# A two-branch linear-attention kernel: folded weights laid by branch, K's PSUM as two tiles, and another order of the first steps

## The chip, the cores and the metric

The kernel runs on one core of a Trainium2 chip. The metric is the device time of one execution in microseconds (us). PE is the matrix engine (PEld its weight loads), DVE the vector engine, ACT the scalar engine, POOL the GpSimd engine, and SP issues the transfers. SBUF is the on-chip memory, PSUM the matrix engine's output memory, eight banks of 512 float32 a partition.

## The reference

Two branches, A and B, of the same form work on the same x (2048 tokens, 448 features, 16 heads of 28). A gate mixes their outputs.

```python
qkv = (x @ wqkv).reshape(B, S, 3, H, Dh).transpose(2, 0, 3, 1, 4)
q, k, v = qkv[0], qkv[1], qkv[2]
pq = einsum("bhsd,hdf->bhsf", q, w_phi)
pk = einsum("bhsd,hdf->bhsf", k, w_phi)
phi_q = concatenate([softmax(pq), softmax(-pq)], -1)
phi_k = concatenate([softmax(pk), softmax(-pk)], -1)
kv = einsum("bhsf,bhsd->bhfd", phi_k, v)
z = einsum("bhsf->bhf", phi_k)
o = einsum("bhqf,bhfd->bhqd", phi_q, kv) / (einsum("bhqf,bhf->bhq", phi_q, z) + 1e-6)
branch = o.transpose(0, 2, 1, 3).reshape(B, S, D) @ wo
out = g * A + (1 - g) * B        # g = sigmoid((x * gate_w).sum(-1))
```

## The kernel before

The 2048 tokens are 16 tiles of 128 (`t`), loaded two at a time. Matrix products are made from a high and a low part of each operand: x, the V weights and the folded weights are each split into a rounded copy ("high", by ACT) and what is left over (`low_part`, a subtraction on DVE or POOL). A projection of one tile and one branch is then 11 matmuls into one PSUM bank (`mms`): the high x with the high and the low weights in four chunks each, and three packed chunks of the low x with the high weights. The order `XT` puts high times high first, the low weights from the fifth matmul, and the low x last.

**Warm-up.** `warm` (L638) issues 10 large and 30 small matmuls of zeros, each of which shows as two instructions in the trace.

**V of tiles 0 and 1.** `v_first` takes the chunks in the order in which they come in. The steps that feed it are `load_x0`, `split_x0`, `load_wv` and `split_wv`. V's banks are VA and VB; tile 1 uses K's two banks instead (`v_bank`).

**Folds.** K and Q go straight from x to the features, so the products of `wqkv` and `w_phi` are made on the chip, in four steps F0 to F3 (`fold(n, low)`: branch `b` is n // 2, `gh` is n % 2). One fold is 32 small matmuls into the four-bank tile F, a transpose by DVE to SBUF, which frees F for the next fold, and then four times (K and Q, chunks `j` 0 and 2) a high copy by ACT and a low part by DVE ("D") or POOL ("P"). Each fold is preceded by `load_wt`: eight transfers on SP and a copy on POOL whose key is `wd`. The results lie in `rk` and `rq`, in which chunk, branch and feature are the axes in this order, and are `wkh`, `wkl`, `wqh`, `wql`.

**The body.** K of a tile (`k_proj` for each branch, `k_soft`) goes to the tile "K" of two PSUM banks, one per branch, and is copied by ACT to SBUF (`pk`). DVE takes the maximum and the minimum, POOL subtracts, ACT takes the exponentials, DVE sums and takes reciprocals, and POOL multiplies. Q (`q_proj`, `q_front`, `q_soft`) goes to the tile "Q"; DVE subtracts the maximum, and the result goes through DRAM to a form in which DVE transposes it. `kv_acc` adds the states of two tiles (T0), V's copies lie in `vs`. At the end the kernel makes the numerators (`num`), divides, gates, and multiplies by `wo` (`out_mm`).

**What sets the order.** The steps are added to a planner (`Plan`) in the order of the generator `steps()`. PE's own order is the order in which its steps are added. For the other engines `order()` makes a list schedule with a cost for each step: a step's due time is the earliest due time of those that need it, less its cost, less its argument `ahead`; of the steps that are ready on an engine the one with the earliest due time goes first. `ahead` is passed on to the steps before it. What the engines then do on the chip is in the planned order, whatever their real times are. The order of the first steps stands in `steps()`, L111 to L114:

```python
    yield from (("V", 3, 0), ("F", 1, "DP"), ("V", 3, 1), ("F", 2, "DP"), ("V", 4, 0), ("F", 3, "DP"), ("later",), ("k", 0, 0), ("V", 4, 1), ("q", 0, 0), ("k", 0, 1), ("ks", 0))
    yield from (("K", 1), ("wo_rows",), ("q", 0, 1), ("qf", 0))
    yield from (("S", 0, JIT % 3 - 1), ("K", 2), ("Q", 1), ("S", 1, (JIT - 1) % 3 - 1), ("k", 3, 0), ("k", 3, 1), ("kv", 0, 1), ("ks", 3), ("V", 5))
```

"V" is a tile's V projection with its copies, "k" one branch of a K projection, "ks" the K features of a tile, "q" and "qf" the same for Q, "S" the second half of Q's features, "kv" the states. `later` closes F and opens the banks of Q, of T0 and of O0.

Most operations are recorded at a helper's line: L266 is `tt` (a two-operand operation of DVE or POOL), L269 `act`, L272 `dma`, L410 the matmuls of `mms`.

Of the kernel before, what the change touches and what calls it, by code (L numbers as in the profile page):

```python
# [10 lines left out]
OP = mybir.AluOpType  # L11
# [13 lines left out]
WARM, SMALL = 10, 30  # L25


class Plan:
# [8 lines left out]
    def add(self, eng, cost, fn, r=(), w=(), lat=0.1, kb=0, two=None, ahead=0.0):  # L37
# [10 lines left out]
        self.steps.append((eng, cost, lat, fn, deps, kb, eng == "POOL" if two is None else two, ahead))  # L48
# [4 lines left out]
    def order(self):  # L53
# [19 lines left out]
        for _ in range(n):  # L73
# [10 lines left out]
            i = min((i for i in can[eng] if ready[i] <= t), key=lambda i: due[i])  # L84
            can[eng].remove(i)
            _, cost, lat, _, _, kb, two, _ = self.steps[i]
# [83 lines left out]
def hedgehog_mix(ctx: ExitStack, tc: tile.TileContext, xd, wv, wkt, wqt, wphi, wo, cmask, cpmask, out):  # L170
# [42 lines left out]
    banks("kv", "left", K=2, VA=1, VB=1)  # L213
# [8 lines left out]
    wkh, wkl = (rk[:, i].rearrange("p (c b f h) -> p c b f h", c=4, b=2, f=FD) for i in range(2))  # L222
    wqh, wql = (rq[:, i].rearrange("p (c b f h) -> p c b f h", c=4, b=2, f=FD) for i in range(2))
# [100 lines left out]
    def split_wv(c, b, low):  # L324
# [4 lines left out]
        low_part(low, D, l, wvr[:, c, lo:hi], h.bitcast(F32), [("wvr", c, b), ("vh", c, b)], [("vl", c, b)], ahead=600.0 - 100 * c if b == 0 else 0.0)  # L329
# [21 lines left out]
    def fold(n, low):  # L351
# [13 lines left out]
        for k, (wh, wl) in enumerate(((wkh, wkl), (wqh, wql))):  # L365
            for j in (0, 2):
                h, l = (x[:, j:j + 2, b, :, gh::2].rearrange("p j f u -> p j u f") for x in (wh, wl))
                s = f[:, k, j:j + 2, :FD].rearrange("p j f u -> p j u f")
                key = "kq"[k]
                add("ACT", 0.9, act(h, s), [ftk[n % 2]], [(key, "h", b, gh, j)], ahead=2.0 * (k == 0))  # L370
                e = "POOL" if low[k] == "P" or low[k] == "M" and j else "DVE"
                add(e, {"DVE": 0.88, "POOL": 1.4}[e], tt(e, l, s, h.bitcast(F32), OP.subtract), [ftk[n % 2], (key, "h", b, gh, j)], [(key, "l", b, gh, j)], two=False)
# [43 lines left out]
    def feat(w, b):  # L416
        return [x[:, :, b].rearrange("p c f h -> p c (f h)") for x in w]
# [7 lines left out]
    def v_bank(t, b):  # L425
        return ("K", b, ("K", b)) if t == 1 else (("VA", "VB")[b], 0, ("VA", "VB")[b])
# [20 lines left out]
    def v_proj(t, b):  # L447
# [4 lines left out]
        v_out(t, b)  # L452
# [9 lines left out]
    def k_proj(t, b):  # L462
        add("PE", 11 * 0.197, mms(t, feat((wkh, wkl), b), "K", b, FO, FZ),
            xkeys(t) + wkeys("k", (b,)), [("K", b)])

    def k_soft(t):
        def p4():
            return fm(bank["K"][:, :, FO:FO + D])
# [13 lines left out]
        put("DVE", 2 * D, lambda: V.tensor_reduce(mh[0], pkh, AX.X, OP.max), [kp], [km[0]])  # L482
        put("DVE", 2 * D, lambda: V.tensor_reduce(mh[1], pkh, AX.X, OP.min), [kp], [km[1]])
        put("POOL", 2 * D, tt("POOL", e4[0], pkh, bc[0], OP.subtract), [kp, km[0]], [ke[0]])
        put("POOL", 2 * D, tt("POOL", e4[1], bc[1], pkh, OP.subtract), [kp, km[1]], [ke[1]])
        for s in range(2):
# [3 lines left out]
            add("DVE", 0.25, lambda s=s: V.reciprocal(sm[:, s], sm[:, s]), [], [("sm", t % 2, s)])  # L490
# [172 lines left out]
    first("DVE", 0.1, lambda: V.memset(bank["K"][:, :, FZ:FZ + H], 0.0), [("K", 0), ("K", 1)])  # L663
# [7 lines left out]
    def later():  # L671
# [10 lines left out]
        for i in range(1, 3):  # L682
            first("POOL", 0.4, lambda i=i: G.memset(eqs[i][:, :, :, :, DH:], 0.0), turned(i - 1))
# [10 lines left out]
    for what, *a in steps():  # L694
        if what == "V":
            for b in a[1:] or (0, 1):
                v_proj(a[0], b)
        elif what == "V01":
# [113 lines left out]
```

## Time and profile before

| | us |
|---|---|
| median of three runs | 342.83 (342.69 to 345.25) |
| the profiled execution | 342.14 |
| its span in the trace | 340.4 |
| PE busy | 332.1 |
| DVE busy | 279.6 |
| POOL busy | 252.2 |
| ACT busy | 143.3 |

The span is what the trace shows from the first instruction to the last; 1.7 us of the execution lie around it. A group of matmuls overlaps in the array, so a group's busy time includes the tail of its last matmul. In the trace the names of tiles stand without their numbers, and an SBUF tile may hold several things in turn: `ret` holds the V weights as loaded, the raw weights of the folds, the K features and the Q features.

### The profile page before, as it was taken

How to read it: one execution, taken by the hardware profiler on the slowest of the kernel's cores; microseconds unless marked ns; L12 is line 12 of the kernel's file. 1: busy time of each engine (PE TensorE's matmuls, PEld its weight loads, DVE VectorE, ACT ScalarE, POOL GpSimd, SP SyncE). 2: the span in 40 equal slices, each digit the busy share in tenths (PEclk: the TensorE clock that was granted, in tenths of full speed). 3: DMA queues.
4: the chain of work that ended last, by engine and by line, in shares of the span. 5: the costliest groups of instructions: out<-in, count | busy, mean ns of one | idle time of the engine just before them, and what ended most of it. 6: DMA issues, size and time to landing. Idle time of an engine off the chain costs nothing.

```text
span 340.4 us, 8927 instructions
## 1 busy us (share of the span) xinstructions
PE 332.1 (98%) x3776; PEld 296.1 (87%) x3776; DVE 279.6 (82%) x335; ACT 143.3 (42%) x219; POOL 252.2 (74%) x212
## 2 busy tenths in 40 slices
PE   8999999999999999999999999999899999999995
PEld 8877889899999999999999998899678888888895
DVE  4547839986797789899988989985799999999970
ACT  4647634462454463546426244342043343433231
POOL 7158365999999799999967985993088778788500
PEclk9999999999999999999999999999999999999999
DMA  7887503612349639848364232396855545241011
GB/s 252 257 212 207 149 1 72 202 56 74 97 158 325 170 107 341 276 145 302 98 221 169 66 111 62 102 351 206 307 178 172 199 156 166 91 179 56 30 54 54
DMA packets 29855, 54.73 MB, mean 161 GB/s; under 512 B 4616, under 2 KB 25464, under 8 KB 27512
## 3 DMA queue, kind: packets, MB, share of 16 engines
q1 hardware_dynamic: 29560, 54.06, 49.1%
q8 instruction: 29, 0.48, 0.6%
q0 software_dynamic: 256, 0.12, 0.1%
q14 instruction: 10, 0.08, 0.1%
HBM read 31.54 MB, written 24.22 MB: 164 GB/s over the span
## 4 chain that ended last, share of the span: by engine, by line
PE 44%; POOL 24%; DVE 14%; issue 9%; DMA 5%; ACT 3%; SPq 1%; POOLq 0%; DVEq 0%; ACTq 0%
PE O L631 21%; POOL ret L266 20%; PE N L583 7%; PE Q L410 5%; PE VB L410 3%; POOL rx L266 3%; PE K L410 3%; DVE ret L546 3%; DVE sm L489 2%; PE VA L410 2%; DVE mx L482 2%; DMA ed<-ret 2%; DMA ret<-in_wv 2%; PE F L358 1%; ACT ret L269 1%
## 5 line engine op out<-in xcount | busy, mean ns | idle before, releaser
L410 PE MATMUL K<-rk,rx 128*128 128x432 f32 x352 | 72.5, 360 | 0.7 <-ACT pk L269 0.6
L410 PE MATMUL Q<-rq,rx 128*128 128x432 f32 x352 | 72.5, 360 | 0.3 <-DVE ru L266 0.3
L631 PE MATMUL O<-rk,rx 128*128 128x448 f32 x336 | 70.4, 368 | 0.0
L410 PEld LDWEIGHTS K<-rk,rx 128*128 128x128 f32 x352 | 65.7, 188 | 5.1 <-ACT pk L269 1.5
L410 PEld LDWEIGHTS Q<-rq,rx 128*128 128x128 f32 x352 | 65.8, 188 | 4.7 <-DVE ru L266 0.9
L631 PEld LDWEIGHTS O<-rk,rx 128*128 128x128 f32 x336 | 62.6, 188 | 8.1 <-issue 1.2
L269 ACT ACTIVATE ret<-ret 128x896 f32<-128x896 f32 x48 | 45.7, 953 | 56.2 <-POOL ret L266 56.0
L266 POOL TENSOR_TENSOR ret<-ret,sm 128x896 f32<-128x896 f32 x32 | 53.9, 1704 | 9.5 <-DVE sm L490 9.5
L489 DVE TENSOR_REDUCE sm<-ret 128x32 f32<-128x896 f32 x32 | 33.8, 1075 | 8.6 <-ACT ret L269 8.6
L546 DVE STREAM_TRANSPOSE ret<-ret 128x2048 f32<-128x2048 f32 x16 | 36.5, 2281 | 1.8 <-POOL ret L266 1.4
L541 DVE TENSOR_REDUCE qsm<-ret 128x32 f32<-128x896 f32 x32 | 33.4, 1053 | 2.7 <-ACT ret L269 2.4
L410 PE MATMUL VA<-rv,rx 128*128 128x450 f32 x154 | 34.4, 371 | 0.0
L410 PE MATMUL VB<-rv,rx 128*128 128x448 f32 x154 | 33.7, 366 | 0.0
L266 POOL TENSOR_TENSOR ret<-qmn,ru 128x896 f32<-128x896 f32 x16 | 28.2, 1762 | 6.9 <-DVE ret L546 4.2
L410 PEld LDWEIGHTS VB<-rv,rx 128*128 128x128 f32 x154 | 28.8, 188 | 3.0 <-issue 0.8
L269 ACT ACTIVATE ret<-ru 128x896 f32<-128x896 f32 x16 | 15.2, 950 | 38.3 <-issue 18.9
L410 PEld LDWEIGHTS VA<-rv,rx 128*128 128x128 f32 x154 | 28.6, 189 | 2.9 <-ACT rk L269 0.4
L266 POOL TENSOR_TENSOR ret<-pk,mx 128x896 f32<-128x896 f32 x16 | 27.3, 1704 | 4.8 <-DVE mx L482 4.7
L266 POOL TENSOR_TENSOR ret<-ret,qsm 128x896 f32<-128x896 f32 x16 | 27.2, 1702 | 0.9
L266 POOL TENSOR_TENSOR ret<-mx,pk 128x896 f32<-128x896 f32 x16 | 27.3, 1705 | 0.0
L603 POOL TENSOR_TENSOR rv<-rv,rd 128x896 f32<-128x896 f32 x14 | 23.8, 1703 | 1.1
L583 PE MATMUL N<-ret,kvt 32*32 32x256 f32 x1024 | 22.7, 385 | 1.6 <-issue 1.6
(92 smaller groups left out, 435.9 us busy)
## 6 DMA issues: line engine op xcount, KB each, us to landing
ed<-ret SPq DMA_DIRECT2D x8, 1024.0 KB
ret<-ed SPq DMA_DIRECT2D x8, 1024.0 KB
qd<-ru SPq DMA_DIRECT2D x64, 112.0 KB
ru<-qd SPq DMA_DIRECT2D x16, 448.0 KB
out<-ret SPq DMA_DIRECT2D x16, 224.0 KB
wod<-wst SPq DMA_DIRECT2D x14, 224.0 KB
rk<-wod SPq DMA_DIRECT2D x2, 1568.0 KB
xraw<-in_xt SPq DMA_DIRECT2D x6, 512.0 KB
```

The lines of the kernel that those rows point to most:

```text
L266: return lambda: ENG[eng].tensor_tensor(val(o), val(a), val(b), op)
L269: return lambda: A.activation(val(o), val(i), f, **k)
L358: nc.tensor.matmul(bank["F"][32 * o:32 * o + 32, q, 256 * l:256 * l + 256], wpd[32 * q:32 * q + DH, b, g], wts[32 * q:32 * q + DH, :, b, g ...
L410: nc.tensor.matmul(bank[name][:, k, lo:hi], x[:, xc, o:o + P], w[l][:, c], start=i == 0, stop=i == len(XT) - 1)
L482: put("DVE", 2 * D, lambda: V.tensor_reduce(mh[0], pkh, AX.X, OP.max), [kp], [km[0]])
L489: put("DVE", 2 * D, lambda s=s, e3=e3: V.tensor_reduce(sm[:, s], e3, AX.X, OP.add), [ke[s]], [("sm", t % 2, s)])
L541: put("DVE", 2 * D, lambda s=s, e3=e3: V.tensor_reduce(qsm[:, s], e3, AX.X, OP.add), [ke[s]], [("qsm", i, s)])
L546: add("DVE", 2.25, lambda: V.transpose(eTf[slot], eq.rearrange("p s a c f -> p (s a c f)")), ke, turned(slot))
L583: nc.tensor.matmul(bank["N"][32 * g:32 * g + 32, r, 2 * b * P:2 * b * P + 2 * P], kvt[32 * r:32 * r + 32, b, s, g], eTp[slots[0] // 2][32 ...
L603: put(eng, 2 * D, lambda: ENG[eng].tensor_tensor(mid["o", n % 3].rearrange("p (c a f) -> p a c f", c=4, a=8), ctv()[:, :, i, :, :DH], rd[: ...
L631: nc.tensor.matmul(bank[pb][:, 0, :D], a, w, start=i == 0, stop=i == len(terms) - 1)
```

## The change

- **Warm-up:** 11 large and 15 small matmuls in place of 10 and 30.
- **Layout:** `rk` and `rq` hold branch, chunk, feature in place of chunk, branch, feature. The slices in `fold` and `feat` follow.
- **K's PSUM:** two tiles of one bank, K0 and K1, in place of one of two banks. `k_soft` copies each branch by itself, for every tile; before, this was so for tile 0 alone.
- **Planner:** a new argument `now` moves a step forward among the ready ones, but is not passed on to the steps before it. The reciprocals of the K sums of tiles 0 and 1 have `now` 20 and 12.
- **First steps:** other `ahead` values for the low parts of x's first two tiles and of V's weights.
- **Folds:** in F1 the low K part of chunk 0 goes to POOL ("N"); F0's low Q part of chunk 2 stays behind `wd` 2; the two memsets of `eqs` on POOL come behind `wd` 3.
- **Order on PE:** V of tile 4, branch 1, goes ahead of K of tile 0, branch 0; V of tile 5, branch 0, goes ahead of the states of tiles 0 and 1, and its copies behind them ("vm" is the projection, "vo" the copies).

```diff
-WARM, SMALL = 10, 30
+WARM, SMALL = 11, 15
...
-            i = min((i for i in can[eng] if ready[i] <= t), key=lambda i: due[i])
+            i = min((i for i in can[eng] if ready[i] <= t), key=lambda i: due[i] - self.steps[i][8])
...
-    yield from (("V", 3, 0), ("F", 1, "DP"), ("V", 3, 1), ("F", 2, "DP"), ("V", 4, 0), ("F", 3, "DP"), ("later",), ("k", 0, 0), ("V", 4, 1), ("q", 0, 0), ("k", 0, 1), ("ks", 0))
+    yield from (("V", 3, 0), ("F", 1, "NP"), ("V", 3, 1), ("F", 2, "DP"), ("V", 4, 0), ("F", 3, "DP"), ("later",), ("V", 4, 1), ("k", 0, 0), ("q", 0, 0), ("k", 0, 1), ("ks", 0))
...
-    yield from (("S", 0, JIT % 3 - 1), ("K", 2), ("Q", 1), ("S", 1, (JIT - 1) % 3 - 1), ("k", 3, 0), ("k", 3, 1), ("kv", 0, 1), ("ks", 3), ("V", 5))
+    yield from (("S", 0, JIT % 3 - 1), ("K", 2), ("Q", 1), ("S", 1, (JIT - 1) % 3 - 1), ("k", 3, 0), ("k", 3, 1), ("vm", 5, 0), ("kv", 0, 1), ("vo", 5, 0), ("ks", 3), ("V", 5, 1))
...
-    banks("kv", "left", K=2, VA=1, VB=1)
+    banks("kv", "left", K0=1, K1=1, VA=1, VB=1)
...
-    wkh, wkl = (rk[:, i].rearrange("p (c b f h) -> p c b f h", c=4, b=2, f=FD) for i in range(2))
+    wkh, wkl = (rk[:, i].rearrange("p (b c f h) -> p b c f h", c=4, b=2, f=FD) for i in range(2))
...
-        low_part("DVE", 2 * P, t[:, 4], xraw[:, 0], f[:, 0], [("x0raw", 0), ("x0h", 0)], [("x0l", 0)], ahead=165.0)
+        low_part("DVE", 2 * P, t[:, 4], xraw[:, 0], f[:, 0], [("x0raw", 0), ("x0h", 0)], [("x0l", 0)], ahead=680.0)
...
-        low_part("DVE", 2 * P, t[64:P, 3], xraw[64:P, 3], f[64:P, 3], [("x0raw", 1)], [("x0h", 3)], ahead=135.0)
-        low_part("DVE", 4 * P, t[:, 5:7], xraw[:, 1:3], f[:, 1:3], [("x0raw", 1), ("x0h", 1), ("x0h", 2)], [("x0l", i) for i in (1, 2)], ahead=140.0)
+        low_part("DVE", 2 * P, t[64:P, 3], xraw[64:P, 3], f[64:P, 3], [("x0raw", 1)], [("x0h", 3)], ahead=660.0)
+        low_part("DVE", 4 * P, t[:, 5:7], xraw[:, 1:3], f[:, 1:3], [("x0raw", 1), ("x0h", 1), ("x0h", 2)], [("x0l", i) for i in (1, 2)], ahead=440.0)
...
-        low_part(low, D, l, wvr[:, c, lo:hi], h.bitcast(F32), [("wvr", c, b), ("vh", c, b)], [("vl", c, b)], ahead=600.0 - 100 * c if b == 0 else 0.0)
+        low_part(low, D, l, wvr[:, c, lo:hi], h.bitcast(F32), [("wvr", c, b), ("vh", c, b)], [("vl", c, b)], ahead=(600.0, 600.0, 400.0, 300.0)[c] if b == 0 else 0.0)
...
-                e = "POOL" if low[k] == "P" or low[k] == "M" and j else "DVE"
+                e = "POOL" if low[k] == "P" or low[k] == "N" and j == 0 else "DVE"
...
-        if t:
-            put("ACT", 2 * D, act(pk, p4), [("K", 0), ("K", 1)], [kp])
-        else:
-            for b in range(2):
-                put("ACT", D, act(pk[:, b], lambda b=b: p4()[:, b]), [("K", b)], [("pk0", b)])
-            plan.hand_over([("pk0", b) for b in range(2)], [kp])
+        for b in range(2):
+            put("ACT", D, act(pk[:, b:b + 1], lambda b=b: fm(bank[f"K{b}"][:, :, FO:FO + D])), [("K", b)], [(*kp, b)])
+        kp = [(*kp, b) for b in range(2)]
...
-            add("DVE", 0.25, lambda s=s: V.reciprocal(sm[:, s], sm[:, s]), [], [("sm", t % 2, s)])
+            add("DVE", 0.25, lambda s=s: V.reciprocal(sm[:, s], sm[:, s]), [], [("sm", t % 2, s)], now=(20.0, 12.0)[t] if t < 2 else 0.0)
...
-            first("POOL", 0.4, lambda i=i: G.memset(eqs[i][:, :, :, :, DH:], 0.0), turned(i - 1))
+            add("POOL", 0.4, lambda i=i: G.memset(eqs[i][:, :, :, :, DH:], 0.0), [("wd", 3)], turned(i - 1))
```

More of the change, by code (lines that the diff above doesn't have):

```diff
@@ L35, in __init__, with add @@
         self.steps, self.writer, self.readers = [], {}, {}
-    def add(self, eng, cost, fn, r=(), w=(), lat=0.1, kb=0, two=None, ahead=0.0):
+    def add(self, eng, cost, fn, r=(), w=(), lat=0.1, kb=0, two=None, ahead=0.0, now=0.0):
         i, deps = len(self.steps), set()
@@ L47, in add @@
             self.writer[k], self.readers[k] = i, set()
-        self.steps.append((eng, cost, lat, fn, deps, kb, eng == "POOL" if two is None else two, ahead))
+        self.steps.append((eng, cost, lat, fn, deps, kb, eng == "POOL" if two is None else two, ahead, now))
     def hand_over(self, old, new, fn=None):
@@ L83, in order @@
             t, eng = best
-            i = min((i for i in can[eng] if ready[i] <= t), key=lambda i: due[i])
+            i = min((i for i in can[eng] if ready[i] <= t), key=lambda i: due[i] - self.steps[i][8])
             can[eng].remove(i)
-            _, cost, lat, _, _, kb, two, _ = self.steps[i]
+            _, cost, lat, _, _, kb, two, _, _ = self.steps[i]
             if two:
@@ L416, in feat @@
     def feat(w, b):
-        return [x[:, :, b].rearrange("p c f h -> p c (f h)") for x in w]
+        return [x[:, b].rearrange("p c f h -> p c (f h)") for x in w]
     def hb(ap):
@@ L425, in v_bank @@
     def v_bank(t, b):
-        return ("K", b, ("K", b)) if t == 1 else (("VA", "VB")[b], 0, ("VA", "VB")[b])
+        return (f"K{b}", 0, ("K", b)) if t == 1 else (("VA", "VB")[b], 0, ("VA", "VB")[b])
     def v_weights(b):
@@ L662, in hedgehog_mix @@
     load_x(1)
-    first("DVE", 0.1, lambda: V.memset(bank["K"][:, :, FZ:FZ + H], 0.0), [("K", 0), ("K", 1)])
+    for b in range(2):
+        first("DVE", 0.1, lambda b=b: V.memset(bank[f"K{b}"][:, :, FZ:FZ + H], 0.0), [("K", b)])
     for i, v in enumerate(vs):
@@ L697, in hedgehog_mix @@
                 v_proj(a[0], b)
+                v_out(a[0], b)
+        elif what in ("vm", "vo"):
+            (v_proj if what == "vm" else v_out)(*a)
         elif what == "V01":
```

21 lines of the change are left out of this document (9 added, 12 removed).

## The prediction

> **What bounds the kernel now.** I read the summary of the page first, then the waits of PE, then two stretches of the table by stretch, then the timeline of the first 70 us.
>
> ```profile
> span 340.4 us, 8927 instructions
> PE 332.1 (98%) x3776; PEld 296.1 (87%) x3776; DVE 279.6 (82%) x335; ACT 143.3 (42%) x219; POOL 252.2 (74%) x212
> PE N L583 <- issue: 1.6, 2, 1.0
> PE K L410 <- ACT pk L269: 0.6, 1, 0.6
> PE F L358 <- DVE ret L363: 0.5, 1, 0.5
> PE T L501 <- POOL ret L266: 0.4, 2, 0.2
> PE VA L442 <- DVE rx L266: 0.3, 1, 0.3
> PE Q L410 <- DVE ru L266: 0.3, 1, 0.3
> 46.00:59.00 13.00, 12.35 (x60) 11.19 (x61) 10.56 (x13) 6.30 (x8) 7.85 (x5) 1.00 0.17 39
> 59.00:172.00 113.00, 112.78 (x1160) 105.26 (x1159) 98.85 (x118) 54.03 (x76) 109.07 (x75) 1.00 0.56 181
> ```
>
> PE is busy for 332.1 of 340.4 us. A wait row gives its total, how often and the longest: here is everything PE waited for after its first instruction, some 3.7 us in six places. So the change cannot win more than these, the extra cost that each leaves behind, and what it saves at the start. The last two rows give, by stretch, the busy time of PE, PEld, DVE, ACT, POOL (count in brackets), then granted clock, DMA share and GB/s. From 59 to 172 us PE idles 0.2 us, but POOL is busy for 109.07 of 113 us as well: two engines are full, and whoever brings PE forward must bring POOL forward too. From 46 to 59 us POOL works only 7.85 of 13 us; there it has 5.15 us to give.
>
> **The change part by part.** A timeline row is start, busy time, engine, line, operation, tiles, count, and in brackets the idle time before and its releaser. The start:
>
> ```profile
> 1.06 4.62 PE L640 MATMUL VB<-zero 128*128 128x128 f32 x20 [1.06 <-DVE zero L649]
> 5.61 0.72 PE L643 MATMUL F<-zero 32*32 32x32 f32 x60
> 6.26 0.47 PE L442 MATMUL VA<-rv,rx 128*128 128x450 f32 x1
> 6.97 0.63 DVE L266 TENSOR_TENSOR rv<-ret,rv 128x450 fp32r<-128x450 f32 x1 [0.68 <-ACT rv L269]
> 9.43 0.36 PE L442 MATMUL K<-rv,rx 128*128 128x450 f32 x1
> 9.52 0.42 DVE L266 TENSOR_TENSOR rx<-xraw,rx 64x256 fp32r<-64x256 f32 x1
> 10.09 0.44 PE L442 MATMUL VA<-rv,rx 128*128 128x450 f32 x1 [0.29 <-DVE rx L266]
> 11.40 2.39 PE L442 MATMUL VB<-rv,rx 128*128 128x448 f32 x11
> ```
>
> *Warm-up.* The 10 large matmuls are 20 instructions from 1.06 to 5.61, 0.23 each; one more adds 0.46 if at that pace. The 30 small are 60 instructions in 0.65; fifteen fewer save about 0.33. Sum +0.13, V01 starting at 6.39; ends: -0.33 (the large one free) and +0.46 (the small ones hide under something); I take the proportional value.
>
> [...]
>
> *Order of the x and V splits.* V01's 16 matmuls from 6.26 to 9.43 go at one each 0.2 us; the next comes only at 10.09, 0.66 later, because DVE makes the low half of x's fourth chunk last, at 9.52. With `ahead` 660 that step goes ahead of V's low parts, behind the copy it needs; DVE has 0.68 us idle ahead of 6.97, and the step takes 0.42. Next late is V's chunk 3, whose low part DVE does behind 6.97, in the row order now two steps before 9.52, so at 9.5; the matmul that needs it comes after 10. Gain 0.46; ends 0 (the planner puts it elsewhere) and 0.6.
>
> ```profile
> 28.15 1.79 PE L358 MATMUL F<-ret,wpd 28*32 28x256 f32 x64
> 29.63 0.93 DVE L266 TENSOR_TENSOR rk<-ru,rk 128x432 fp32r<-128x432 f32 x1 [1.53 <-ACT rk L269]
> 29.87 2.50 PE L410 MATMUL VA<-rv,rx 128*128 128x450 f32 x11
> 30.46 2.31 DVE L363 STREAM_TRANSPOSE ret<-F 128x2048 f32<-128x2048 f32 x1
> 31.18 2.66 POOL L266 TENSOR_TENSOR rq<-ru,rq 128x432 fp32r<-128x432 f32 x2 [0.36 <-ACT rq L269]
> 32.70 1.93 DVE L266 TENSOR_TENSOR rk<-ru,rk 128x432 fp32r<-128x432 f32 x1
> 32.83 1.79 PE L358 MATMUL F<-ret,wpd 28*32 28x256 f32 x64 [0.46 <-DVE ret L363]
> 34.55 2.44 PE L410 MATMUL K<-rk,rx 128*128 128x432 f32 x11
> 39.52 1.67 DVE L266 TENSOR_TENSOR rk<-ru,rk 128x432 fp32r<-128x432 f32 x2
> 41.45 4.47 PE L410 MATMUL K<-rk,rx 128*128 128x432 f32 x22
> 42.49 2.65 POOL L266 TENSOR_TENSOR rq<-ru,rq 128x432 fp32r<-128x432 f32 x2 [4.31 <-ACT rq L269]
> ```
>
> *Folds.* F3 (32.83) waits for the transpose of F2, which starts at 30.46 although F2's matmuls end at 29.87: DVE is on F1's first K low part (0.93). "NP" gives that part to POOL, so the transpose starts near 29.95 and ends 2.31 later, at 32.26: F3 0.5 earlier. V4's first half ends at about 32.2 and is late next, so no more than 0.6; the other end is 0, should DVE still have another part there. POOL gets one 1.33 us operation (2.66 for two). It delays F1's Q parts on POOL, which nobody reads before Q0, behind K0's first half (34.55) and V4's second. DVE's 0.93 becomes 1.93 while POOL's pair runs, so the two engines do hold each other up: one more POOL part can cost DVE up to 1.33. DVE's last K parts (39.52, done at 41.19) are read by the K matmuls from 41.45, which will come about 1 us sooner, but their low halves only from the fifth of eleven matmuls, 0.8 later, and DVE has shed 0.93. I take 0; ends -0 and +0.8. [...]
>
> The two memsets of `eqs` and the fold's copy `wd 2` only change places in POOL's queue; none of the moved steps issues a transfer on SP or POOL. POOL idles 4.3 us ahead of 42.49, which hides them; without that cover they cost at most their length. Putting V4's second half ahead of K0 is neutral in work; it hides the last folds better: 0.2 from the restarts between 34.55 and 41.45 (ends 0 and 0.3).
>
> ```profile
> 41.45 1.75 ACT L269 ACTIVATE rq<-ru 128x432 fp32r<-128x432 f32 x2 [2.01 <-PE Q L410]
> 45.96 0.54 ACT L269 ACTIVATE pk<-K 128x448 f32<-128x448 f32 x1 [2.38 <-PE K L410]
> 46.54 1.09 DVE L482 TENSOR_REDUCE mx<-pk 128x32 f32<-128x896 f32 x1 [5.35 <-ACT pk L269]
> 46.56 2.47 PE L410 MATMUL K<-rk,rx 128*128 128x432 f32 x11 [0.63 <-ACT pk L269]
> 50.36 0.90 ACT L269 ACTIVATE pk<-K 128x896 f32<-128x896 f32 x1
> 55.80 4.59 PE L410 MATMUL Q<-rq,rx 128*128 128x432 f32 x22
> 58.64 0.98 DVE L490 RECIPROCAL sm<-sm 128x32 f32<-128x32 f32 x4
> 59.13 6.68 POOL L266 TENSOR_TENSOR ret<-ret,sm 128x896 f32<-128x896 f32 x4 [2.00 <-DVE sm L490]
> 65.87 0.99 PE L501 MATMUL T<-ret,vs 128*29 128x56 f32 x64 [0.22 <-POOL ret L266]
> 66.79 2.53 PE L410 MATMUL VA<-rv,rx 128*128 128x450 f32 x11
> 207.96 4.59 PE L410 MATMUL Q<-rq,rx 128*128 128x432 f32 x22 [0.27 <-DVE ru L266]
> ```
>
> *Two K tiles.* K0's second half ends near 43.6, but ACT's copy of it starts at 45.96, when the K matmuls of tile 1 in the other bank are done too: with one tile of two banks the copy waits for both. So the 22 matmuls from 41.45 take until 46.56, 5.11 us. They are busy for 4.47, of which the last one's tail of some 0.16 (0.36 busy against 0.2 a step, the row at 9.43) could overlap the next: 4.31. With two tiles the copy starts near 43.7, and the wait goes: 0.8, and I add 0.1 for the slower first matmul after a wait, 0.9; ends 0.6 (the wait's own row) and 1.0. It also starts the whole chain of tile 0 (46.54) 2.2 us sooner, with the shift 3 or more. Later tiles pay two copies of 0.54 for one of 0.90, 0.18 on ACT, which is 42% busy: nothing on PE, if the half copies hold nobody up behind them (a rival).
>
> *Then.* K2 at 51.31 and Q1 at 55.80 come behind short restarts for the copy at 50.36 and DVE's Q front; both releasers come 2 to 3 us sooner: 0.5 together; ends 0 and 0.6.
>
> *Fold layout.* ACT's last Q parts wait 2.01 for PE's Q matmuls of the other branch, which are interleaved with them in one range; laid by branch they need not. POOL, 4.31 idle, gets them sooner. Nobody waits for the result: 0. Copies and operands have the same shapes.
>
> *Reciprocals first, V5 ahead of kv.* Four reciprocals run together at 58.64, POOL idling 2.00 for them; with `now` they follow their sums, and POOL's four products (6.68) end 4 us sooner, near 62. V5's first half ahead of the states gives 2.2 more. The state stall (0.22, with restart 0.4) goes; ends 0.2 and 0.4. Next late would be the Q front, if DVE did the sums first.
>
> **Sum.** +0.13 - 0.46 - 0.5 - 0.2 - 0.9 - 0.5 - 0.4 = -2.83 us at 66.79; behind it nothing changes if POOL moves along, and N's 1.6 of "issue" stays. The profiled execution took 342.14 us (span 340.4) and would take 339.3; the median of the runs is 342.83, 0.69 above it, so 340.0.
>
> **The rivals.**
> *More than that.* POOL gains more (about 4) than PE (2.8), so the late waits at 207.96 (0.27, with restart 0.4) and at the states near 216 (0.2, with restart 0.4) go too. For it: both wait on the DVE and POOL chain that the change starts earlier. Against: between 172 and 207 that chain already has slack, and the order there is planned anew. 340.0 - 0.8 = 339.2.
>
> *Given back.* POOL, full from 59 to 172, doesn't start earlier after all (its products keep waiting for DVE's sums), and PE arrives earlier only to wait at the states. Then V01 and the folds bring nothing behind 60 us; up to 2.4 of the gain is lost: 341 to 342.6. Against: POOL's 5.15 idle us.
>
> *Slower.* In-order ACT stands at a half copy for a K bank while an exponential that POOL's full queue needs stands behind it. A half is 2.2 us of matmuls; at 0.5 us for each of 13 tiles from tile 3 on, 6.5 are lost against 2.8: 346.5. It decides from 0.22 a tile upwards. Against: ACT has half its time free.
>
> *Clock.* V01 runs at half clock if the clock rises later: 22 matmuls at 0.2 more, +4.4, 344.4. Against: the warm-up is no shorter. [...]
>
> **How the numbers follow.** Forecast 0.41 (own range 339.3 to 340.7), more than that 0.29, given back 0.21, slower 0.06, clock 0.03. A measurement of this kernel tells about 1% from no change, 3.4 us: 339.4 is the line. Faster by over 1% is "more" and a few hundredths of the forecast, 0.33; slower by over 1% 0.06; the rest 0.61. The range takes in "more" with the warm-up's lower end, 338.7, and "given back" to 342.4; it leaves out the last two rivals and the edges.
>
> **What would show it.** V01 without a gap; F3 without its wait; the second K copy right behind the second half of K0, and no PE wait on it; reciprocals apart; no wait at the states. The forecast is wrong if PE shows new waits behind 66 us, for POOL or the Q front, or if F3's wait stays.

## The result, and the profile after

The diff above is an excerpt. Of what it leaves out, one line that the list above it doesn't name sets an order: in `fold` the high copies of K have `ahead` 6.0 in place of 2.0. No run varies that line alone.

| | before | after |
|---|---|---|
| median of 14 runs each, us | 342.73 (340.85 to 345.25) | 339.68 (338.24 to 341.85) |
| the profiled execution | 342.14 | 339.24 |
| its span | 340.4 | 337.4 |

The ratio of the times is 0.992, 95% interval 0.9896 to 0.9945: 2.7 us less, by less than 1%. The prediction said 340.0 for the median and 339.3 for the profiled execution. But the 2.9 us of the trace came in other places than the prediction had them, so the places come first.

From the page of the changed kernel, the summary, and then from its waits of PE (total, times, longest):

```profile
span 337.4 us, 8903 instructions
PE 329.8 (98%) x3748; PEld 296.6 (88%) x3748; DVE 279.2 (83%) x335; ACT 144.4 (43%) x234; POOL 254.7 (75%) x213
PE Q L410 <- DVE Q L672: 1.2, 1, 1.2
PE O L625 <- issue: 1.0, 1, 1.0
PE Q L410 <- DVE ru L266: 0.8, 1, 0.8
```

Of the six waits of before, those on `pk`, on the transpose `ret`, on `ret` at the states and on `rx` are gone. The wait for a Q front has grown from 0.3 to 0.8, "issue" has fallen from 1.6 to 1.0, and the longest, at L672, is new.

Where PE stands at the same piece of work is read from the starts in the two timelines. The last column sums the prediction's terms up to that point.

| PE's work | before | after | difference | predicted |
|---|---|---|---|---|
| VB behind `v_first` | 11.40 | 11.03 | -0.37 | -0.33 |
| F3 | 32.83 | 32.05 | -0.78 | -0.83 |
| Q of tile 0, first branch ("Q0") | 39.22 | 39.68 | +0.46 | -1.03 |
| Q, second branch, behind 33 matmuls of K | 48.86 | 48.38 | -0.48 | -1.93 |
| K of tile 3 | 60.23 | 59.15 | -1.08 | -2.43 |
| K behind the first states | 71.38 | 69.85 | -1.53 | -2.83 |
| Q of the wait `ru` ("the late Q") | 207.96 | 206.89 | -1.07 | -2.83 |
| K behind the states near 215 | 216.83 | 215.34 | -1.49 | -2.83 |
| first N | 238.63 | 237.10 | -1.53 | -2.83 |
| second N | 247.40 | 244.29 | -3.11 | -2.83 |
| last O | 319.50 | 316.55 | -2.95 | -2.83 |

The first 70 us brought 1.5 us, not 2.8, and the loss stands in one line, between F3 and Q0 (1.24 lost where 0.2 was to be won). The other half of the gain came at the first N, where the prediction had nothing.

The start and the folds, from the timeline of the changed kernel (start, busy, engine, line, operation, tiles, count, and in brackets the idle time before and its releaser):

```profile
5.87 0.86 DVE L266 TENSOR_TENSOR rx<-xraw,rx 128x256 fp32r<-128x256 f32 x2
6.39 0.51 PE L442 MATMUL VA<-rv,rx 128*128 128x450 f32 x1
...
30.97 3.37 POOL L266 TENSOR_TENSOR rq<-ru,rq 128x432 fp32r<-128x432 f32 x2
31.92 1.20 DVE L266 TENSOR_TENSOR rk<-ru,rk 128x432 fp32r<-128x432 f32 x1
32.05 1.79 PE L358 MATMUL F<-ret,wpd 28*32 28x256 f32 x64
33.05 4.10 DVE L266 TENSOR_TENSOR rk<-ret,rk 128x432 fp32r<-128x432 f32 x2
34.80 3.59 POOL L266 TENSOR_TENSOR rq<-ret,rq 128x432 fp32r<-128x432 f32 x2
37.06 2.30 DVE L363 STREAM_TRANSPOSE ru<-F 128x2048 f32<-128x2048 f32 x1
39.45 0.09 DVE L672 MEMSET Q<- 128x32 f32 x1
39.68 2.40 PE L410 MATMUL Q<-rq,rx 128*128 128x432 f32 x11 [1.25 <-DVE Q L672]
41.91 6.62 PE L410 MATMUL K<-rk,rx 128*128 128x432 f32 x33
```

The fourth chunk of x now stands in the pair at 5.87, and V01 runs without its gap. F3 runs without its wait. But behind it DVE makes the two K low parts of F2 (33.05), which take 4.10 where one alone takes 0.93 (in the trace of before the two of F2 took 0.95 and 1.34, the second one behind F3's transpose), while POOL's pairs beside them take 3.37 and 3.59 instead of 2.66: each engine is held up while the other works. F3 was done at 33.84 and its transpose begins only at 37.06. F's banks are Q's banks: the zeros of Q wait for that transpose, and Q0 for the zeros. From 41.91 the 33 K matmuls run through; before, 22 and 11 of them stood around a wait of 0.63.

The first states and the late Q in the changed kernel, and two stretches of its table by stretch (length, busy time of PE, PEld, DVE, ACT, POOL, then granted clock, DMA share, GB/s):

```profile
56.48 5.14 POOL L266 TENSOR_TENSOR ret<-ret,sm 128x896 f32<-128x896 f32 x3
65.81 1.78 PE L495 MATMUL T<-ret,vs 128*29 128x56 f32 x128
206.89 4.56 PE L410 MATMUL Q<-rq,rx 128*128 128x432 f32 x22 [0.82 <-DVE ru L266]
46.00:59.00 13.00, 13.00 (x68) 12.46 (x68) 10.65 (x14) 6.47 (x10) 10.92 (x7) 1.00 0.21 57
59.00:172.00 113.00, 113.00 (x1162) 105.64 (x1161) 97.47 (x118) 54.43 (x85) 105.53 (x74) 1.00 0.56 179
```

POOL took 3.1 us of work into the stretch from 46 to 59 (10.92 in place of 7.85), its last product of the first states ends at 61.62 in place of 65.81, and all 128 matmuls of the states run in one row.

The first two groups of the numerators, N, first in the trace of before and then in that of the changed kernel:

```profile
238.63 2.71 PE L583 MATMUL N<-ret,kvt 32*32 32x256 f32 x123
242.31 0.62 PE L583 MATMUL N<-ret,kvt 32*32 32x256 f32 x5 [0.98 <-issue]
247.40 2.16 PE L583 MATMUL N<-ret,kvt 32*32 32x256 f32 x100
250.15 0.71 PE L583 MATMUL N<-ret,kvt 32*32 32x256 f32 x28 [0.59 <-issue]
```

```profile
237.10 2.75 PE L577 MATMUL N<-ret,kvt 32*32 32x256 f32 x128
244.29 2.75 PE L577 MATMUL N<-ret,kvt 32*32 32x256 f32 x128
248.05 4.25 PE L625 MATMUL O<-rk,rx 128*128 128x448 f32 x20 [1.00 <-issue]
```

Before, the first N stops behind its 123rd matmul and the second behind its 100th. After, only one stop is left, and it stands at the end of the second N. Counted from the start, 2517 and 2644 matmul records lie ahead of the two stops of before, and 2644 ahead of the one of after. With the new warm-up there are 28 less (3748 against 3776), so the 2517th is now the first of the second N, behind a Q whose 22 matmuls take 4.5 us, and no longer the 123rd of a row of 128 that takes 2.7.

### The profile page after: what moved, and what is told of

The parts are those of the page before. It is cut to its first block, busy times and chain, and to the rows that moved or that the text cites. A ratio compares the mean times of both kernels' runs of the same rounds, so it can differ in the third digit from the quotient of the medians.

```text
span 337.4 us, 8903 instructions
## 1 busy us (share of the span) xinstructions
PE 329.8 (98%) x3748; PEld 296.6 (88%) x3748; DVE 279.2 (83%) x335; ACT 144.4 (43%) x234; POOL 254.7 (75%) x213
## 4 chain that ended last, share of the span: by engine, by line
PE 89%; DVE 5%; issue 2%; POOL 1%; DMA 1%; ACT 1%; DVEq 0%; ACTq 0%; POOLq 0%
PE O L625 21%; PE Q L410 18%; PE K L410 17%; PE VA L410 9%; PE VB L410 9%; PE N L577 6%; PE T L495 4%; PE VB L634 2%; POOL ret L266 1%; PE F L358 1%; PE K L442 1%; DVE rk L266 1%; DMA ru<-qd 1%; PE VA L442 1%; DVE ru L363 1%
## 5 line engine op out<-in xcount | busy, mean ns | idle before, releaser
L269 ACT ACTIVATE pk<-K 128x448 f32<-128x448 f32 x32 | 17.0, 540 | 18.5 <-PE K L410 17.0
```

Source lines behind the costliest of these rows:

```text
L269: return lambda: A.activation(val(o), val(i), f, **k)
```

## The experiments

Three theories and their rivals. *A:* PE's stops in N are tied to counts of its own instructions, so the warm-up alone moved them; the rival is that PE came to N at another time. *C:* Q0's wait is made by the K low part that went to POOL ("NP"): one more POOL part, by which DVE is blocked. *D:* it is made by DVE's order, F2's second low part standing ahead of F3's transpose. Later *E:* the late Q's wait is DVE's order too. "Before" was timed again beside each group of runs (342.5, 341.97 and 342.38 us), the changed kernel beside the last group alone, so a time is compared by its ratio to before.

### The warm-up by itself, both ways

`a_warm_old` is the changed kernel with the old warm-up, `b_warm_new` the kernel of before with the new one.

```diff
-WARM, SMALL = 11, 15
+WARM, SMALL = 10, 30
```

> The changed kernel with the old warm-up, 10 large and 30 small matmuls; nothing else differs. In the changed kernel's trace the 1.35 us hole in the first numerator group N is gone, and one of 1.38 us stands at the end of the second. Theory A: these holes are PE waiting for its own instructions, which come in 16 KB transfers, and they lie at fixed counts of PE instructions; the new warm-up has 28 matmuls fewer in the trace and so moves the later work against these counts. Then the old warm-up brings back the hole of about 1.35 us in the first N group (and one near 1.0 in the second), V01 starts 0.1 us sooner, and the span is 1.0 to 1.5 us longer than the changed kernel's 337.4, so 338.4 to 338.9. Theory B: the holes depend on the traffic of the body, which the folds and the two K tiles changed. Then the first N group stays without a hole and the span is 337.2 to 337.5.

> The kernel before with the new warm-up alone, 11 large and 15 small matmuls. Theory A (holes lie at fixed counts of PE instructions): the hole of 1.35 us in the first N group goes, the one in the second stays at 1.0 to 1.4, V01 starts 0.13 us later; span 339.2 to 339.6 against 340.4. Theory B (holes come from the traffic of the body): both holes stay, span 340.4 to 340.6.

Measured: `a_warm_old` 341.79 us, ratio to before 0.997 (0.9937 to 1.0002); `b_warm_new` 340.86 us, ratio 0.9957 (0.9925 to 0.9988). The N of `a_warm_old`, and then of `b_warm_new`:

```profile
237.22 2.71 PE L577 MATMUL N<-ret,kvt 32*32 32x256 f32 x123
241.18 0.62 PE L577 MATMUL N<-ret,kvt 32*32 32x256 f32 x5 [1.25 <-issue]
246.26 2.16 PE L577 MATMUL N<-ret,kvt 32*32 32x256 f32 x100
248.94 0.71 PE L577 MATMUL N<-ret,kvt 32*32 32x256 f32 x28 [0.52 <-issue]
```

```profile
238.68 2.75 PE L583 MATMUL N<-ret,kvt 32*32 32x256 f32 x128
245.89 2.75 PE L583 MATMUL N<-ret,kvt 32*32 32x256 f32 x128
249.25 3.01 PE L631 MATMUL O<-rk,rx 128*128 128x448 f32 x14 [0.61 <-issue]
```

With the old warm-up the stops are back behind the 123rd and the 100th matmul, although PE comes to N at 237.22, as in the changed kernel (237.10). With the new one they are gone from there, although PE comes at 238.68, as before (238.63). So the count decides and not the time: A. (A count alone doesn't make a stop: 2517 makes none in `h_small0`, and neither does 2771, the next at the same distance, in before and in the changed kernel. The last section has the numbers.) The warm-up alone makes the kernel of before faster by 0.43%, 1.5 us (0.4 to 2.6), half of the whole change; the other half, without it, is 0.3%, and its interval reaches to none.

In `b_warm_new`, with the old order of the splits, V01 has no gap either: it started 0.13 later and its first two matmuls ran slower (0.3 us together), so PE came to the late x chunk at 10.08, and DVE had made it by 9.66 (9.94 in the trace of before). The 0.46 of the prediction is real in the trace of before, but a start that is 0.4 later takes it away.

### Q0's wait: without the POOL part, and with another order on DVE

`c_dp` gives F1's K low part back to DVE; `d1_defer_j2` keeps it on POOL, but puts F2's second K low part behind F3's transpose (F3 adds it, with the transpose's key as one more to wait for).

```diff
-    ... ("F", 1, "NP"), ...
+    ... ("F", 1, "DP"), ...
```

> The changed kernel with F1's low K part of chunk 0 back on DVE (DP in place of NP). In the changed kernel PE waits 1.25 us at Q0 for the memset of Q on DVE, which comes behind the transpose of F3, and that comes at 37.1 behind two low K parts of F2 that took 4.1 us beside POOL's low Q parts. Theory C: the extra part on POOL pushes POOL's low Q parts onto DVE's low K parts, and the two engines block each other. Then with DP the two low parts of F2 take under 3 us, the transpose of F3 starts by 36.3, the wait at Q0 falls under 0.6 us, while F3 again waits some 0.4 us for F2's transpose. Theory D: it is the order on DVE alone (both low parts of F2 ahead of F3's transpose). Then the wait at Q0 stays at 1 us or grows by 0.9, as DVE has one part more. Span 337.0 by C, 338.0 by D.

```diff
-                add(e, {"DVE": 0.88, "POOL": 1.4}[e], tt(e, l, s, h.bitcast(F32), OP.subtract), [ftk[n % 2], ...
...
+                if (n, k, j) == (2, 0, 2):
+                    kept.append(low_step)
...
```

> The changed kernel with F2's second low K part put behind F3's transpose on DVE, as in the kernel before; nothing else is moved by hand. Theory D (the order on DVE makes the wait at Q0): the transpose of F3 starts some 2 us sooner, near 35.0, Q0 starts near 38.4 and the wait of 1.25 us goes; K's second half of tile 0 may then wait a little for F2's and F3's last low parts. PE is 0.8 to 1.2 us earlier at the fifth V tile than in the changed kernel (V's first half at 62.3 to 62.7 against 63.47). Theory C (blocking between DVE and POOL): the low parts stay slow, and what Q0 gains is lost at K's second half; V's first half of tile 5 stays at 63.2 or later.

Measured: `c_dp` 340.44 us, ratio 0.993 (0.9895 to 0.9964); `d1_defer_j2` 340.87 us, ratio 0.9927 (0.9897 to 0.9957). The same place in `c_dp`, and then in `d1_defer_j2`:

```profile
33.80 1.79 PE L358 MATMUL F<-ret,wpd 28*32 28x256 f32 x64 [0.45 <-DVE ret L363]
...
35.49 0.94 DVE L266 TENSOR_TENSOR rk<-ret,rk 128x432 fp32r<-128x432 f32 x1
36.36 2.30 DVE L363 STREAM_TRANSPOSE ru<-F 128x2048 f32<-128x2048 f32 x1
...
40.23 2.40 PE L410 MATMUL Q<-rq,rx 128*128 128x432 f32 x11
```

```profile
33.32 2.09 DVE L266 TENSOR_TENSOR rk<-ret,rk 128x432 fp32r<-128x432 f32 x1
35.32 2.31 DVE L365 STREAM_TRANSPOSE ru<-F 128x2048 f32<-128x2048 f32 x1
39.01 2.39 PE L419 MATMUL Q<-rq,rx 128*128 128x432 f32 x11 [0.32 <-DVE Q L681]
```

Without the POOL part F2's first low part takes 0.94, the transpose follows it at once, Q0 loses 0.2 at its start, and F3 waits 0.45 as before. The edit changes two things here: the planner also put F2's second low part behind the transpose again (38.59). So `c_dp` by itself doesn't part C from D; `d1_defer_j2` varies the order alone. From F2 to Q0 it is 11.12 us (29.11 to 40.23) against 11.88 in the changed kernel (27.80 to 39.68): with "NP" F3 wins 0.4 and Q0 loses 1.2, 0.76 net. With the POOL part kept and the order mended, F3 doesn't wait and Q0 comes 20.94 us behind F0 (18.07) and not 21.89 behind it (17.79): 0.95 sooner. So both theories hold a part: beside the moved POOL queue DVE's subtraction is 2.09 long, and the order, which the planner changed when the part moved to POOL, lets two of them stand ahead of the transpose.

Neither made the kernel faster as a whole. `c_dp` waits 0.86 for POOL at the states near 81, and its stop at N's end is 1.5 of "issue" in place of 1.0. `d1_defer_j2` is 0.67 ahead of the changed kernel at V of tile 5 (62.80 against 63.47), yet the late Q waits 1.18 in place of 0.82, the stop at N's end is longer (1.8 of "issue" in place of 1.0), and its last O starts at 317.16 against 316.55.

### K's PSUM as one tile again, and the old layout

```diff
-    banks("kv", "left", K0=1, K1=1, VA=1, VB=1)
+    banks("kv", "left", K=2, VA=1, VB=1)
... (and the lines that name these banks)
-    wkh, wkl = (rk[:, i].rearrange("p (b c f h) -> p b c f h", c=4, b=2, f=FD) for i in range(2))
+    wkh, wkl = (rk[:, i].rearrange("p (c b f h) -> p c b f h", c=4, b=2, f=FD) for i in range(2))
... (the same for wqh, wql; and their slices)
```

The first pair of lines is `e_one_k` (each branch still copied by itself), the second `f_layout`; both are the changed kernel otherwise, with one run and profile each.

> The changed kernel with K's PSUM again one tile of two banks, still copied branch by branch; nothing else differs. If the two tiles are what took away the wait of the copy of K0's second half for both banks' matmuls, the wait on PE in K of tile 1 comes back, and the 33 K matmuls of tiles 0 and 1 take 7.4 us in place of 6.46; in later tiles each first-half copy may wait for the second half too, and PE then waits for it at the next K where no Q or V lies between. V's first half of tile 5 starts 0.8 to 1.2 us later than 63.47. Rival: the halved copy or the planner's new order made the gain; then the 33 K matmuls stay at 6.5.

> The changed kernel with the old layout of the folded weights (chunk, branch, feature); the order on each engine is the same. Prediction's theory: ACT's last high Q parts wait again for PE's Q matmuls of the other branch, POOL's low Q parts come later, and nobody waits for them: PE within 0.2 us of the changed kernel at tile 5's V (63.47) and in the span's first 200 us. Rival: with PE earlier than before, the high parts of F2 and F3 (ACT) now also wait behind K0's first half, which reads the same range, and K0's second half waits for them: 0.5 to 2 us lost there.

Measured: 342.37 and 339.36 us. The wait on the K copy is back in `e_one_k`:

```profile
46.80 0.54 ACT L269 ACTIVATE pk<-K 128x448 f32<-128x448 f32 x1 [3.31 <-PE K L410]
47.39 0.86 PE L410 MATMUL K<-rk,rx 128*128 128x432 f32 x3 [0.63 <-ACT pk L269]
```

The 33 K matmuls take 7.39 (42.28 to 49.67) against 6.46 in the changed kernel, 0.93 more, and from there to K of tile 3 another 0.4 are lost in restarts: 1.35, where the prediction had 0.9 and 0.5. In `f_layout` PE stands within 0.2 us of the changed kernel from Q0 on (63.49 against 63.47 at V of tile 5, last O 316.71 against 316.55): in this pair of profiles the layout is worth nothing.

### The reciprocals and V of tile 5 put back

```diff
-    ... ("vm", 5, 0), ("kv", 0, 1), ("vo", 5, 0), ("ks", 3), ("V", 5, 1))
+    ... ("kv", 0, 1), ("ks", 3), ("V", 5))
...
-            ... [("sm", t % 2, s)], now=(20.0, 12.0)[t] if t < 2 else 0.0)
+            ... [("sm", t % 2, s)])
```

> The changed kernel with the reciprocals of tiles 0 and 1 without their precedence and V of tile 5 wholly behind the states of tiles 0 and 1, as before. Prediction's theory: the stall between the two halves of the states comes back, 0.3 to 0.5 us, as the products on POOL end later; V of tile 5 ends (fourth K group starts) 0.3 to 0.5 us later than 69.85. Rival: the chain of tile 0 starts 1.7 us sooner anyway (44.8 against 46.5), which alone removes the stall: no difference over 0.15 us there.

Measured: 343.78 us, one run. The first and the last states that waited:

```profile
64.01 1.98 PE L495 MATMUL T<-ret,vs 128*29 128x56 f32 x128
236.11 0.99 PE L495 MATMUL T<-ret,vs 128*29 128x56 f32 x64 [1.69 <-POOL ret L266]
```

At the first states only 0.2 us are lost (1.91 from 64.01 to the next group, against 1.71), half of the 0.4 that the prediction gave to this part. Most of the other 4.4 us come later: the late Q waits 1.66 and the states at 236 another 1.69, in a plan that the planner made anew. One run and a whole new plan don't say what the part is worth there.

### No small matmuls at all

`h_small0` is the changed kernel with `SMALL = 0`, 30 matmul records less, so that the count 2644 falls into the first O. The count 2517 now lies 31 matmuls into the second N.

> The changed kernel with a warm-up of 11 large matmuls and no small one: 30 PE matmul records fewer. Theory A (PE waits for its own instructions at fixed counts): the count 2643, at which every trace so far shows a hole of 0.9 to 2.2 us, moves from the end of the second N group 30 matmuls into the first output group O, where PE spends 0.2 us a matmul and the transfer of instructions keeps up: no hole in either N group, 1.0 to 1.4 us less; V01 starts up to 0.3 us sooner, if its data are there. Span 335.8 to 336.4 against 337.4. Theory B (the holes belong to the first N groups): a hole of 1 us or more stays in an N group, span 337.1 or more. If the clock had not risen by V01 without the small ones, V01's first matmuls would take 0.4 us each and the gain would be less by 0.2 each.

Measured: 341.62 us, ratio 0.9971 (0.9942 to 0.9999). Both N run in 2.69 us, with no stop. The stop at N's end went with its count (A again), and the count 2517 makes none where it stands now. But the time is not better: the late Q waits 1.94, and then runs slowly. The wait from the timeline, and a stretch from the table:

```profile
208.26 6.15 PE L410 MATMUL Q<-rq,rx 128*128 128x432 f32 x22 [1.94 <-DVE ru L266]
209.30:212.80 3.50, 3.50 (x12) 3.21 (x11) 3.50 (x6) 0.00 (x0) 2.20 (x2) 0.51 0.54 128
```

The granted clock is 0.51 from 209.3 to 212.8; the 22 matmuls take 5.99 us instead of 4.40. Six of the ten executions of `h_small0` have a mean granted clock of 0.993 or 0.994, as the profiled one has, and took 341.25 to 344.25 us; the four at 0.998 to 1.000 took 339.15 to 342.15. The medians of the two are 1.7 us apart, close to the 1.59 that the slow Q costs, so most executions lost to the clock about what the missing stop had won.

### The late Q's wait, and all three losses at once

`after_again` is the changed kernel once more. `i1_qfront` is it with one more dependence on DVE: the minimum of Q's soft part of tile 10 comes behind the Q front of tile 11 (a key `qf` is added to the front for this). `i2_all` has this, the order of `d1_defer_j2`, and no small matmuls.

```diff
-        put("DVE", 2 * D, lambda: V.tensor_reduce(qmn, ..., AX.X, OP.min), [kt], [kn])
+        put("DVE", 2 * D, lambda: V.tensor_reduce(qmn, ..., AX.X, OP.min), [kt, *([("qf", 11, b) for b in range(2)] if k == 10 else [])], [kn])
```

> The changed kernel once more, as the measure for the two beside it: median near 339.7, profiled span near 337.4, the Q0 wait of about 1.2, the Q12 wait of about 0.8, N0 without a hole and a hole of about 1.4 at N1's end. If the N0 hole is a matter of fixed counts (theory A), it is at the same matmul records again, whatever the time.

> The changed kernel with DVE's minimum of Q's soft part for tile 10 (L529) made to come behind the Q front of tile 11. Theory E (the 0.82 that PE waits at Q12 is DVE's order: that minimum stands waiting for its copy, with the Q front of tile 11 behind it): Q12's wait falls below 0.3 and Q12 starts about 0.8 earlier relative to K14; the gain lasts if the states near 215 find their products in time: span 336.6, last O at 315.8 in place of 316.55. Rival (DVE's chain is full there, the order doesn't matter): the wait at Q12 stays, or the same 0.8 turns up at the states near 213 to 216 or at Q14: span 337.4 or more.

> The changed kernel with three edits: F2's second K low part behind F3's transpose (Q0's wait of 1.25 goes, -0.9), the minimum behind the Q front (Q12's wait of 0.8 goes) and no small warm-up matmuls (no hole at N1's end, -1.4). If the three losses are independent (each has its own cause on PE): span 334 to 335.5, time 336.5 to 338. Rival (DVE's and POOL's chain between 60 and 207 us gives back what PE gains in front): Q12 or the states wait as much as PE was brought forward, and only the hole's 1.4 is won: span 336. If PE idles more than 2 us near 206 and the granted clock falls behind it, as with no small matmuls alone, Q12 takes 6 in place of 4.4 and the span is above 338.

Measured, all beside the same runs of before: `after_again` 340.08 us, ratio 0.9944 (0.9915 to 0.9973); `i1_qfront` 340.52, 0.9935 (0.9907 to 0.9963); `i2_all` 339.93, 0.9933 (0.9906 to 0.9961). The three can't be told apart. In `i1_qfront`:

```profile
205.87 4.46 PE L410 MATMUL Q<-rq,rx 128*128 128x432 f32 x22
244.81 2.75 PE L577 MATMUL N<-ret,kvt 32*32 32x256 f32 x128 [1.23 <-DMA ret<-ed]
```

E is right about the place: the late Q starts without a wait and 1.02 us sooner. The rival is right about the time: the second N now waits 1.23 for a transfer (Q features coming back from DRAM, issued at 234.07 against 233.03), and the last O starts at 317.39. In `i2_all` the two late waits are these:

```profile
192.19 1.09 DVE L538 TENSOR_REDUCE qmn<-ru 128x32 f32<-128x896 f32 x1 [1.51 <-DMA ru<-qd]
207.15 4.58 PE L419 MATMUL Q<-rq,rx 128*128 128x432 f32 x22 [1.42 <-DVE ru L266]
```

PE is 1.17 us ahead of the changed kernel at V of tile 5 (62.30 against 63.47), 0.34 ahead at the K matmuls before the late Q (201.25 against 201.59), and 0.26 behind at the late Q. Between, POOL isn't ready at two of the states (PE idles 0.2 at each), and DVE stands 1.51 us at a minimum whose input comes through DRAM (190.71 in the changed kernel, behind 0.90). Another wait of 0.60 for POOL comes at the states near 232. The stop at N's end is gone, but PE comes to N 1.04 later (238.14): span 338.0. The rival of that expectation holds.

`after_again` shows how far one profile of one kernel carries. Its span is 340.4, 3.0 more than in the first profile of the same kernel, and 1.4 of it come from the start:

```profile
20.55 1.04 POOL L314 CAST rx<-xraw 128x1024 fp32r<-128x1024 f32 x1 [2.36 <-DMA xraw<-in_xt]
24.29 1.08 POOL L349 COPY ret<-ret 128x256 f32<-128x256 f32 x1
25.43 1.36 PE L358 MATMUL F<-ret,wpd 28*32 28x256 f32 x48 [0.56 <-POOL ret L349]
```

A load of x came at 20.55; in the first profile this cast started at 18.54 and the fold's copy at 22.27. The copy stands behind the cast in POOL's queue, so it is 2.0 us later and F1 stops in its middle. From then on PE is 1.4 us behind (V of tile 5 at 64.89), the late Q waits 1.25, and "issue" at N's end is 1.8. Across all 13 profiles this cast starts between 17.65 and 20.55; the stop in F1 is there in `c_dp` too, which had the cast at 20.43, so that of `c_dp` isn't the edit's.

## Why the prediction was right, and which of its steps were not

The time came as forecast, 340.0 against 339.68, and the sum of the trace too, -2.83 against -2.95. But two steps failed, by 1.4 us each, and they offset each other. That is luck: nothing in the prediction ties the one to the other.

**Right, step by step.** *Order of the x and V splits and warm-up:* -0.37 against -0.33. `a_warm_old`, which has the new order with the old warm-up, has VB at 10.91, -0.49 where the prediction had -0.46, and V01 starts at 6.27 against 6.39, the 0.12 of the warm-up. But over the eleven other profiles VB begins anywhere from 10.80 to 11.31, 11.20 in the second profile of the changed kernel and 11.31 in `b_warm_new`, so that the sum fits to 0.04 is luck too. *F3:* -0.41 against -0.5. *Two K tiles:* -0.94 between Q0 and the next Q half against -0.9, and 0.93 back in `e_one_k`. *K2 and Q1 restarts:* -0.60 against -0.5, in `e_one_k` back with the wait. *States:* -0.45 against -0.4; `g_late` shows 0.2 of it, so half may belong to the earlier start. *Layout:* 0, and the rival on the slow side, ACT standing at the half copies, left no trace: in no run with two K tiles does PE wait for a copy of K. POOL did move along, as the forecast needed.

**The step that failed: "one more POOL part can cost DVE up to 1.33 ... I take 0; ends -0 and +0.8".** It cost +1.24 at Q0, where the order on PE was to bring -0.2 too, so this place was 1.4 worse than the sum. The effect was named, and its size was taken as nothing. The prediction read its price off one DVE part, 1.93 beside a POOL pair where one alone took 0.93, and assumed one such meeting. With POOL's queue moved, three DVE parts met two POOL pairs (1.20 and 4.10 beside 3.37 and 3.59). It took DVE's order as it was, too, while the planner put F2's second low part ahead of F3's transpose. And it looked for the reader in the wrong place: not the K matmuls that read the low parts, 0.8 behind their start, but F3's transpose, which stands behind these parts on DVE's queue and frees the banks that Q0 needs. `d1_defer_j2` (0.95 back by the order alone) and `c_dp` (0.76 back without the part, and with the old order) show it.

**The step that failed: "N's 1.6 of 'issue' stays".** It took "issue" for a fixed property of N. In these traces it hangs on how many instructions PE had run before, and the prediction itself had counted the 28 that the warm-up drops (20 and 60 against 22 and 30; here 3776 against 3748). It gave +0.13 to the warm-up and nothing behind it. `a_warm_old` and `b_warm_new` show that the new warm-up is worth about -1.5, all at N.

**The rival of the clock.** No run shows its 4.4, V01's 22 matmuls all at half clock. In `b_warm_new`, whose record of the clock begins at 7.12, V01's first two matmuls stand 0.54 and 0.30 us ahead of the next ones (6.39, 6.93, 7.23), in the changed kernel, with the record from 6.49 on, 0.34 and 0.21 (6.39, 6.73, 6.94): 0.3 lost.

**A slip that moved nothing.** The upper end of "given back" is 340.0 + 2.4 = 342.4, not 342.6; the range was set by 342.4.

**"Behind it nothing changes if POOL moves along".** Nearly so in this trace: -1.53 at 70 us and -1.53 at the first N. Between them 0.5 was given back at the late Q (0.82 for 0.27) and won again at the states near 215, whose wait is gone. That is a half of the rival "more than that" (the states) and a little of "given back" (the late Q). The experiments say more: whoever takes another 0.7 to 1.2 us off the start has lost half of it (`d1_defer_j2`, 0.33 left) or all of it (`i2_all`, 0.26 behind) when the late Q starts, and whoever mends the late Q (`i1_qfront`) loses it at N. So the 2.8 of the first 70 us, had they come, would probably not have lasted; no run had exactly that, so this is argued from these three.

What stays open: why the return of Q's difference from DRAM, the transfer behind DVE's minimum near 190 us, comes up to 1.8 us later in one variant than in another (the minimum that waits for it starts at 190.71 in the changed kernel, at 192.19 in `i2_all` and at 192.55 in `h_small0`). In `after_again`, the same plan with PE 1.4 behind, it starts at 192.01. No run held all but the transfer fixed.

## What to carry to other kernels

A gap that the profile puts down to "issue" may hang on the number of instructions before it: here 28 matmul records less at the start left one of two such stops in N and moved it (`b_warm_new`), so compare such gaps by count before giving them to a change. When work moves to an engine beside which another one slows down (two DVE parts 4.10 us in place of 1.9 beside POOL's), price every meeting of the two, and look for the readers not only of the result but of whatever stands behind it in the slowed queue. And where several engines are nearly full (here PE 113.00 and POOL 105.53 of 113 us), a wait that is mended may come back at the next one, as the 0.82 of the late Q came back as 1.23 at the second N in `i1_qfront`: the gain counts from the last group of work, over several runs, since one profile of this kernel differs from the next by up to 3 us (337.4 and 340.4).

## What the runs showed of the hardware

*PE stops at certain counts of its own instructions.* The page of the changed kernel has the instruction queues:

```profile
q8 instruction: 29, 0.48, 0.6%
```

29 packets with 0.48 MB, 16 KB each. At both stops of before, PE goes on about 1.3 to 1.5 us behind the end of such a packet (in the trace's record of transfers, 240.10 to 241.02 and on at 242.31; 247.73 to 248.69 and on at 250.15). Eleven of the 13 profiles have such stops, 13 in all, each at the count 2517 or 2644, and at each PE goes on 1.25 to 1.51 us behind a packet's end (the one of `i1_qfront`, at 248.82, the page puts down to ACT). The stops are 127 matmul records apart, each with its weight load, which makes 254 instructions. The page doesn't say whose instructions the packets hold; if they are PE's, 3748 matmul records and as many loads in 29 packets are 258 a packet, an estimate from these numbers that is near the distance of the counts. Among the matmuls 0.2 us apart PE shows no such stop (the waits of before and of the changed kernel have no other "issue"), while the 128 small ones of an N and their loads are through in 2.69 us (`h_small0`). A count alone doesn't make a stop: the 13 stand behind 100, 123 or 128 small matmuls in a row. The count 2517 in `h_small0`, behind 31 of them, makes none, and neither does 2771, the next one at the same distance, which lies 57 matmuls into the third N of before and 85 into that of the changed kernel. There the packet is through early: in the changed kernel the last one ends at 255.56, and PE comes to 2771 near 258.2. That the packets cause the stops is read from this order in time and from the counts; nothing but the counts was varied, and what sets the start of a packet stays open.

*DVE and POOL stretched each other.* In the changed kernel two subtractions on DVE (33.05) took 4.10 us in place of 1.9 (0.93 for one alone, 29.63 in before), two on POOL beside them (34.80) 3.59 in place of 2.66 (31.18 in before): in this pair of queues both lose.

*The clock fell in the middle of one profile.* In `h_small0` PE was idle for 1.94 us ahead of 208.26, and from 209.35 the granted clock was half for 3.41 us (0.51 in the table from 209.3 to 212.8); the 22 matmuls there took 5.99 us instead of 4.40. In `g_late`, `i2_all` and `after_again`, with waits of 1.66, 1.42 and 1.25 us at the same place, it stayed full. Whether the length of the wait decides was not shown: no run varies it alone. At the start the record of the clock begins between 3.9 and 7.1 us in the 13 profiles (5.53 in that of before, 6.49 in that of the changed kernel), and the first matmuls of V01 are slower by 0.3 in one run and not in another. Ahead of the record the table shows 1.00 (0 to 1 us in both, 6.39 to 7.20 in `b_warm_new`), which doesn't say what was granted there. The stretch at full clock was 331.09, 334.51 or 337.92 us in the 12 profiles without a fall (331.09 in the changed kernel, 334.51 in before), whatever the kernel did within it: from one value to the next it is 3.41 us, as long as the fall in `h_small0`. Why it comes in these steps was not shown.
